# Third batch's list as 19 small blocks, transforms paced eight blocks ahead of their list, gate columns copied by ScalarE, four output buffers

## The chip, the cores and the metric

The kernel runs on one core of one Trainium2 chip. TensorE (PE, with its weight loads as PEld), VectorE (DVE), ScalarE (ACT), GpSimd (POOL) and SyncE (SP) each work through an instruction queue of their own; semaphores order them against each other. SP issues most DMAs, POOL the indirect ones. The metric is the device time of one execution in microseconds (us), lower is better.

## What is computed

A two-dimensional Fourier transform of 8 batches of 2496 tokens by 256 columns, of which the real part goes on; then a mixture of 8 experts, where each token goes through the one expert with the highest gate value. Cut to what matters:

```python
X = np.fft.fft(np.fft.fft(x, axis=1), axis=2).real     # (8, 2496, 256)
x = X.reshape(8 * 2496, 256)
logits = x @ w_gate + modality_bias[modality_id]       # 8 experts
e_idx = np.argmax(logits, axis=1)
gate_w = softmax(logits)[np.arange(N), e_idx]
for e in range(8):
    mask = e_idx == e
    h = np.maximum(x[mask] @ w1[e], 0.0)               # 256 -> 1024
    out[mask] = gate_w[mask, None] * (h @ w2[e])       # 1024 -> 256
```

## The kernel before

**Transforms.** One generator, `stream`, emits all batches in small steps, about 29 to a batch. `fold` adds and subtracts mirrored inputs on VectorE, and `fold_add` squares them on ScalarE (L371, `XM` with `nst`) for a norm, which TensorE sums (L386). `stage1` multiplies into PSUM (`psf`, four buffers) and empties it into `T1`. `stage23` runs over 11 groups: a second transform into `T2`, a third into `psf`, whose 256 columns are emptied into a row tile `rp` (`evac`, L486 on ScalarE and L487 on VectorE) and whose 16 gate columns go to `Lg` (L560). `route` picks each token's expert and its place in that expert's region of the DRAM buffer `xd`. A batch fills four `rp` tiles of up to three groups. Batches 0, 1, 2, 4 and 6 (counted from 0) take them from one pool of `RPB` buffers, the others from a second pool. Each batch's rows go to `xd` by 22 indirect DMAs on POOL (L670, from `rp` and from its mirror `rm`); `paced` and `trickle` spread these between other POOL work.

**Expert blocks.** `block` takes S tokens of one expert, 256 or 128. SP loads the expert's two weight halves (L987, L988; 2.05 MB together; only if the expert differs from the one already in that slot; three slots in turn), the tokens transposed (`xT`, L990) and their output addresses (`ig`, L993). TensorE multiplies into `psm` (L1006); ScalarE takes the ReLU into `H` (L1011), and VectorE the remainder (L1012), each in tiles of 512 columns. TensorE multiplies `H` with the second weights into `pso` (L1024, one buffer). ScalarE scales 128 tokens at a time into an output tile `ob` (L1030, two buffers), and POOL scatters it to the output (L1031). The first half of a block is issued ahead of the second half of the block before it.

**Lists.** First come eight blocks of 256 out of batch 0, one for each expert, while the expert weights are still being prepared ("w", "s" and "b" steps of the string `SEQ` mix weight, transform and block steps; 12 of the 16 half blocks lie in it, the other four behind it). Then come lists: list R holds full blocks of the tokens of batches 0 to R-1 that are not yet taken, as many as are certain to exist whatever the routing: n = (R x 2496 - taken - 8 (S-1)) // S. List 2 has blocks of 128, lists 3 to 8 blocks of 256; what is left goes in a final list of 128. `table` works out on VectorE which expert each block has. With these inputs the numbers of blocks are 15 of 128, then 5, 10, 10, 10, 9 and 10 of 256, then 22 that run of the final list's 24.

**Order.** `fft_moe` emits the transform steps between blocks: `pts` gives, for a count `at` of blocks (in units of 256 tokens), how far the transforms are to be, and `knots` interpolates. Batch b is due one unit before list b begins. A scheduler then fixes each engine's queue from its own estimate of readiness, so what stands in a queue can run ahead of the order in which it was emitted, and a small edit can move rows far from it.

Of the kernel before, what the change touches and what calls it, by code (L numbers as in the profile page):

```python
# [30 lines left out]
ROW = 516  # L31
RW = 516
CH = 3
RPB = 6
RPL = 4
HIP = ()
HIV = ()
# [19 lines left out]
NSLOT = 2  # L57
NS2 = 3
LEAD = 2
EARLY = -1  # L60
FIRST = 2
WAB = 4
WFB = 1
# [162 lines left out]
class Kernel:  # L226
# [288 lines left out]
    def stage23(self, b):  # L515
# [8 lines left out]
        for g in range(G + 1):  # L524
# [19 lines left out]
            if g > 0:  # L544
                T2 = T2s[g - 1]
                ps3 = self.psf.tile([P, 512], F32, name="psf")
                for j, cols in enumerate((slice(0, 145), slice(145, 280))):
                    if hl:
                        for k, (a, w) in enumerate(HL):
                            nc.tensor.matmul(ps3[0:M3, cols], self.e3h[:, a, j, :], T2[:, w, cols], start=k == 0, stop=k == 2)  # L550
                    else:
                        nc.tensor.matmul(ps3[0:M3, cols], self.e3[:, j, :], T2[:, cols], start=True, stop=True)  # L552
                j = (g - 1) % CH
                if j == 0:
                    pool, n = (self.rows, RPL) if b >= SPB and b % 2 else (self.rt, RPB)
                    self.rp.append(pool.tile([M3, CH, RW], I16, name="rp", bufs=n))
                row = self.rp[-1].bitcast(F16)[:, j, 0:512].rearrange("p (h s c) -> p h s c", h=2, c=64)
                seg = ps3[0:M3, 0:288].rearrange("p (s c) -> p s c", c=72)
                self.evac(row, seg[:, :, 0:64], 2.0 ** -20 if hl else self.inv[0][:M3])
                nc.vector.tensor_copy(Lg[:, g - 1], seg[:, 0:3:2, 64:72])  # L560
            yield

    def modality(self):
# [399 lines left out]
    def block(self, S, ti, i, o=0, n=0, ex=None):  # L963
# [62 lines left out]
        gs = p.tile([P, NT], F32, name=f"gs{S}", bufs=3)  # L1026
        V.tensor_scalar(gs, ig[:, :, 1], w2[:, 4 * F:4 * F + 2].bitcast(F32), None, ALU.mult)  # L1027
        for tg in range(NT):
            ob = p.tile([P, D], F32, name="ob", bufs=2)
            self.ob = nc.scalar.activation(ob, po[:, tg, :], AF.Identity, scale=gs[:, tg:tg + 1]).ins  # L1030
            ins = nc.gpsimd.indirect_dma_start(  # L1031
                out=t["out"], out_offset=bass.IndirectOffsetOnAxis(ap=ig.bitcast(I32)[:, tg, 0:1], axis=0),
# [32 lines left out]
def fft_moe(ctx, tc, t):  # L1065
# [32 lines left out]
        next(st, None)  # L1098
    for _ in blk:
        k.paced()  # L1100
        for i in range(3):
            next(st, None)
            k.paced()
    k.started = True

    R0 = FIRST
    size = lambda R: P if R == R0 else 256
    starts, taken = {R0: 0}, k.ntaken
    for R in range(R0, B):
        n = (R * N - taken - E * (size(R) - 1)) // size(R)  # L1110
        starts[R + 1] = starts[R] + n * size(R) / 256
        taken += size(R) * n
    pts = [(0, k.pos)] + [(starts[b] + EARLY, b + 1) for b in range(SPB, B)]
    at = 0
    k.slots = lambda b: int(2 * (starts[b + 1] - LEAD - at))
    tab = k.table(size(R0), False, R0)
    for R in range(R0, B + 1):
        blk, nxt = k.blocks(size(R), tab, R), None
        for _ in blk:
# [3 lines left out]
            if R < B and nxt is None and at >= starts[R + 1] - LEAD:  # L1123
                while k.ready < R:
                    next(st)
                nxt = k.table(256, False, R + 1)
        tab = nxt
    run_all([k.blocks(128, k.table(128, True))])

# [54 lines left out]
```

## Time and profile before

| | |
|---|---|
| median of 3 runs | 1083.2 us (1081.33 to 1083.68) |
| profiled execution | 1081.88 us, span 1080.1 us |
| TensorE busy | 1007.7 us of the span |
| VectorE busy | 552.8 us |
| ScalarE busy | 446.8 us |
| GpSimd busy | 373.3 us |
| moved by DMA | 254.89 MB, mean 236 GB/s |

In the profile a row of a timeline gives start and length in us, engine, line, operation, what it writes and reads, the number of instructions and, in brackets, how long the engine stood idle just before and what released it. Matmuls overlap in the pipeline, so the distance from one start to the next says more than a row's length. A row of the waits gives who waited for whom, the total in us, how often, and the longest. A wait off the path that sets the end costs nothing.

### The profile page before, as it was taken

Reading aid. Unit: us, or ns where it says so; the run is one execution under the profiler, and the core shown is the slowest. Engines: PE = TensorE matmul, PEld = TensorE weight load, DVE = VectorE, ACT = ScalarE, POOL = GpSimd, SP = SyncE. Lnnn points to the kernel's source line nnn. Section 1 sums busy time; section 2 is a strip of 40 time slices with the busy share of each in tenths; the row PEclk is TensorE's granted clock in tenths of the full one; section 3 lists DMA queues with packets and bytes.
Section 4 is the critical chain, followed back from the end, with each engine's and each line's share of the span. In section 5 each row is a group of like instructions: output and inputs, shape, how many; then the busy total and the mean of one; then the engine's idle time right before and its main releaser. Section 6 shows DMA issues by size and latency. Waiting matters only on the chain.

```text
span 1080.1 us, 26648 instructions
## 1 busy us (share of the span) xinstructions
PE 1007.7 (93%) x10128; PEld 910.1 (84%) x10128; DVE 552.8 (51%) x1620; ACT 446.8 (41%) x882; POOL 373.3 (35%) x351
## 2 busy tenths in 40 slices
PE   6776879889998999999999999999999999999996
PEld 5656868779888988889899999888888888899985
DVE  4878888978887442363565334732222222222221
ACT  6755767744644333333443343332323233233221
POOL 0072482861243334343334333345543112121111
PEclk9897989999999999999999999999999999999998
DMA  9667987799497979877878595849976886797663
GB/s 348 246 227 247 308 270 240 260 295 332 135 287 226 305 240 292 225 235 249 252 221 259 178 251 156 244 126 287 298 215 197 244 272 183 222 242 204 163 156 105
DMA packets 156484, 254.89 MB, mean 236 GB/s; under 512 B 118364, under 2 KB 121317, under 8 KB 136125
## 3 DMA queue, kind: packets, MB, share of 16 engines
q1 hardware_dynamic: 136973, 210.96, 66.7%
q0 software_dynamic: 19376, 42.16, 11.8%
q8 instruction: 82, 1.34, 0.5%
q14 instruction: 53, 0.43, 0.1%
HBM read 231.59 MB, written 60.48 MB: 270 GB/s over the span
## 4 chain that ended last, share of the span: by engine, by line
PE 64%; issue 13%; DMA 9%; DVE 5%; ACT 4%; POOL 3%; SPq 1%; POOLq 0%; ACTq 0%; DVEq 0%
PE psm L1006 29%; PE pso L1024 28%; DMA XM<-x 3%; DMA out<-ob,ig 3%; POOL out L1031 2%; PE psf L550 2%; PE psf L532 1%; PE psf L506 1%; ACT wj L812 1%; DVE XM L368 1%; DMA xd<-rp,dsti 1%; PE psf L508 1%; POOL xd L670 1%; DMA wa<-w 1%; DVE w L838 1%
## 5 line engine op out<-in xcount | busy, mean ns | idle before, releaser
L1024 PEld LDWEIGHTS <-H 128*128 128x128 f16 x3864 | 376.1, 98 | 55.7 <-ACT H L1011 10.3
L1031 POOL DMA_INDIRECT out<-ob,ig x161 | 166.6, 1035 | 583.2 <-ACT ob L1030 503.4
L1012 DVE SCALAR_TENSOR_TENSOR H<-psm,H 128x512 f16<-128x512 f32 x322 | 218.4, 686 | 282.7 <-ACT H L1011 281.4
L1006 PE MATMUL psm<-xT,w 128*128 128x256 f16 (+1 forms) x3216 | 315.0, 256 | 13.5 <-DMA xT<-xd 6.7
L1024 PE MATMUL pso<-w,H 128*128 128x256 f16 x2616 | 308.0, 273 | 10.7 <-ACT H L1011 9.0
L1006 PEld LDWEIGHTS <-w 128*128 128x128 f16 x3216 | 268.9, 99 | 41.3 <-issue 11.7
L1011 ACT ACTIVATE H<-psm 128x512 f16<-128x512 f32 x322 | 190.5, 597 | 239.8 <-PE psm L1006 238.7
L1030 ACT ACTIVATE ob<-pso,gs 128x256 f32<-128x256 f32 x161 | 70.7, 471 | 282.1 <-PE pso L1024 239.4
L1006 PE MATMUL psm<-xT,w_y 128*128 128x256 f16 (+1 forms) x1440 | 135.3, 251 | 0.5 <-DVE H L1012 0.4
L670 POOL DMA_INDIRECT xd<-rp,dsti x88 | 104.7, 1190 | 84.5 <-DVE sp_i L863 53.7
L1024 PE MATMUL pso<-w_y,H 128*128 128x256 f16 x1152 | 133.3, 273 | 0.0
L1006 PEld LDWEIGHTS <-w_y 128*128 128x128 f16 x1440 | 117.0, 98 | 11.0 <-issue 1.2
L670 POOL DMA_INDIRECT xd<-rm,dsti x88 | 93.3, 1060 | 28.5 <-issue 25.2
L487 DVE SCALAR_TENSOR_TENSOR T<-psf,T 120x280 f16<-120x280 f32 (+2 forms) x95 | 43.2, 461 | 56.3 <-ACT T L486 55.9
L1027 DVE TENSOR_SCALAR gs<-ig,w 128x2 f32<-128x2 f32 (+1 forms) x67 | 15.2, 227 | 63.2 <-DMA ig<-xd 63.2
L486 ACT ACTIVATE T<-psf 120x280 f16<-120x280 f32 (+2 forms) x95 | 38.6, 421 | 15.4 <-PE psf L532 10.2
L812 ACT ACTIVATE wj<-wa 128x1024 f16<-128x1024 f32 x32 | 34.3, 1072 | 9.5 <-DMA wa<-w 9.4
L550 PE MATMUL psf<-T,pack 120*117 120x145 f16 x330 | 31.8, 224 | 4.8 <-DVE T L487 3.0
L368 DVE TENSOR_TENSOR XM<-XM 128x1280 f32<-128x1280 f32 (+2 forms) x18 | 24.1, 1338 | 23.2 <-DMA XM<-x 23.2
L552 PEld LDWEIGHTS psf<-T,pack 120*117 120x117 f32 x132 | 19.4, 188 | 17.0 <-ACT T L482 11.2
L552 PE MATMUL psf<-T,pack 120*117 120x145 f32 (+1 forms) x132 | 23.4, 300 | 11.1 <-ACT T L482 7.5
L532 PE MATMUL psf<-pack,T 128*120 128x144 f16 (+1 forms) x330 | 32.2, 229 | 1.3 <-DVE Lg L560 1.3
(197 smaller groups left out, 772.8 us busy)
## 6 DMA issues: line engine op xcount, KB each, us to landing
w<-w SPq DMA_DIRECT2D x67, 1028.0 KB
w<-w SPq DMA_DIRECT2D x67, 1024.0 KB
w_y<-w SPq DMA_DIRECT2D x30, 1028.0 KB
w_y<-w SPq DMA_DIRECT2D x30, 1024.0 KB
XM<-x SPq DMA_DIRECT2D x14, 1280.0 KB
wa<-w SPq DMA_DIRECT2D x16, 1024.0 KB
out<-ob,ig POOLq DMA_INDIRECT x161, 6.3
w<-w_x SPq DMA_DIRECT2D x2, 1028.0 KB
```

The source lines that it names most:

```text
L487: self.mark = self.nc.vector.scalar_tensor_tensor(dst[:, 1], ps, scale, dst[:, 0], ALU.mult, ALU.subtract).ins
L532: nc.tensor.matmul(oh, T1[h][:, a, g, :], self.m2h[h][:, w], start=h + k == 0, stop=h * k == 2, skip_group_check=True)
L550: nc.tensor.matmul(ps3[0:M3, cols], self.e3h[:, a, j, :], T2[:, w, cols], start=k == 0, stop=k == 2)
L552: nc.tensor.matmul(ps3[0:M3, cols], self.e3[:, j, :], T2[:, cols], start=True, stop=True)
L670: i = self.nc.gpsimd.indirect_dma_start(out=self.t["xd"], out_offset=bass.IndirectOffsetOnAxis(ap=at, axis=0), in_=row, in_offset=None, bo ...
L812: nc.scalar.activation(jk, x, AF.Square, accum_out=st[:, i:i + 1])
L1006: l1 = nc.tensor.matmul(ps[:, q, :], w1v[:, h, kt, ft], xT[:, xs, :], start=k == 0, stop=k == 5).ins
L1011: nc.scalar.activation(H[:, 0, f0:f0 + NF, :], ps, AF.Relu)
L1012: self.mark = V.scalar_tensor_tensor(H[:, 1, f0:f0 + NF, :], ps, 0.0, H[:, 0, f0:f0 + NF, :], ALU.max, ALU.subtract).ins
L1024: nc.tensor.matmul(po[:, tg, :], H[:, hh, ft, tg * P:(tg + 1) * P], w2v[:, wh, ft, :], start=k == 0, stop=k == 23)
L1030: self.ob = nc.scalar.activation(ob, po[:, tg, :], AF.Identity, scale=gs[:, tg:tg + 1]).ins
L1031: ins = nc.gpsimd.indirect_dma_start(out=t["out"], out_offset=bass.IndirectOffsetOnAxis(ap=ig.bitcast(I32)[:, tg, 0:1], axis=0), in_=ob, i ...
```

## The change

Four edits of the kernel and the settings that go with them:

- Lists below number 4 use blocks of 128 (`SMALL`), so list 3 does as well as list 2. By the formula it has 19 blocks where it had 5 of 256, and the lists behind it have 6, 9, 10, 10 and 10, the final one 23, of which 21 run.
- Batch b is due eight units before list b+1 begins (`AHEAD`), where it was due one unit before list b began. Behind `SEQ`, one transform step follows each half block of the first eight, where three did.
- The gate columns are copied out of PSUM by ScalarE.
- `ob` has four buffers; the pool of row tiles has five where it had six.

```diff
-RPB = 6
+RPB = 5
...
-EARLY = -1
+AHEAD = 8
+SMALL = 4
...
-                nc.vector.tensor_copy(Lg[:, g - 1], seg[:, 0:3:2, 64:72])
+                nc.scalar.copy(Lg[:, g - 1], seg[:, 0:3:2, 64:72])
...
-            ob = p.tile([P, D], F32, name="ob", bufs=2)
+            ob = p.tile([P, D], F32, name="ob", bufs=4)
...
     for _ in blk:
         k.paced()
-        for i in range(3):
-            next(st, None)
-            k.paced()
+        next(st, None)
+        k.paced()
...
-    size = lambda R: P if R == R0 else 256
+    size = lambda R: P if R < SMALL else 256
...
-    pts = [(0, k.pos)] + [(starts[b] + EARLY, b + 1) for b in range(SPB, B)]
+    pts = [(0, k.pos)] + [(starts[b + 1] - AHEAD, b + 1) for b in range(SPB, B)]
...
-                nxt = k.table(256, False, R + 1)
+                nxt = k.table(size(R + 1), False, R + 1)
```

In the changed file the lines behind the settings are numbered one higher. Two places in ScalarE's queue show how the order moved. The first is where the third of the first eight blocks is put out (`ob` with `gs_1750`); `H_1798` is the ReLU of the block behind it, `w_1_107` a half of a prepared weight, `wj` a weight norm, `T_1576` and the like results of the second transform. Before:

```order
L837 ACTIVATE w_1_107<-wa,wsc 128x2048
L542 COPY T_1576<-psf 120x280
L486 ACTIVATE rp<-psf,xsc 117x256
L542 COPY T_1591<-psf 120x280
L812 ACTIVATE wj,wst<-wa 128x1024
L1030 ACTIVATE ob<-pso,gs_1750 128x256 x2
L1011 ACTIVATE H_1798<-psm 128x512
L812 ACTIVATE wj,wst<-wa 128x1024
L1011 ACTIVATE H_1798<-psm 128x512
```

The same place with the change:

```order
L487 ACTIVATE rp<-psf,xsc 117x256
L543 COPY T_1591<-psf 120x280
L1031 ACTIVATE ob<-pso,gs_1750 128x256 x2
L1012 ACTIVATE H_1798<-psm 128x512 x2
L487 ACTIVATE rp<-psf,xsc 117x256
L543 COPY T_1605<-psf 120x280
L1012 ACTIVATE H_1798<-psm 128x512
L475 ACTIVATE XM<-Pt,xsc 128x640
L475 ACTIVATE XM<-Qt,xsc 128x640
L813 ACTIVATE wj,wst<-wa 128x1024
L487 ACTIVATE rp<-psf,xsc 117x256
L561 COPY Lg<-psf 117x16 x2
```

The next block's ReLU stands right behind the two outputs in both; the weight norm that parted its first two tiles has moved behind the third, and copies of gate columns now stand in the queue, two at a time, behind the row tiles.

The second place is late in list 2, where the transforms of batch 5 stand between small blocks; `H_4511` is the ReLU of the list's twelfth block before, `H_4596`, `H_4719` and `H_4862` those of its last three with the change, and `T_6202` and `T_7345` the first of that batch's second transform. Before:

```order
L486 ACTIVATE T_6202<-psf 120x280
L486 ACTIVATE T_6282<-psf 120x280
L486 ACTIVATE T_6303<-psf 120x280
L486 ACTIVATE rp<-psf 117x256 x2
L486 ACTIVATE T_6412<-psf 120x280
L486 ACTIVATE rp<-psf 117x256
L371 ACTIVATE XM,nst<-XM 128x1280
L486 ACTIVATE T_6499<-psf 120x280
L486 ACTIVATE T_6520<-psf 120x280
L1011 ACTIVATE H_4511<-psm 128x512 x2
L1030 ACTIVATE ob<-pso,gs_4646 128x256
L486 ACTIVATE T_6625<-psf 120x280
```

With the change:

```order
L487 ACTIVATE T_7345<-psf 120x280
L487 ACTIVATE T_7524<-psf 120x280
L487 ACTIVATE T_7588<-psf 120x280
L487 ACTIVATE T_7700<-psf 120x280
L372 ACTIVATE XM,nst<-XM 128x1280
L1012 ACTIVATE H_4596<-psm 128x512 x2
L1031 ACTIVATE ob<-pso,gs_4676 128x256
L487 ACTIVATE T_7758<-psf 120x280
L372 ACTIVATE XM,nst<-XM 128x1280
L1012 ACTIVATE H_4719<-psm 128x512 x2
L1031 ACTIVATE ob<-pso,gs_4819 128x256
L1012 ACTIVATE H_4862<-psm 128x512 x2
```

Ahead of the first block shown stand four results and one set of squares, where six results, three row tiles and the squares stood; the next result and the second squares lie a block further on, and the row tiles have moved behind the blocks shown.

## The prediction

> **What bounds the kernel now.** I read first the page's forty slices, then the busy time by stage, then who waited for whom, and last the timeline at the waits. Durations and sums stand against the profiled execution: 1081.88 us, of which its span is 1080.1 us. The median of the runs shown, 1083.2 us, lies 1.3 us above it.
>
> ```profile
> PE   6776879889998999999999999999999999999996
> DVE  4878888978887442363565334732222222222221
> ...
> 0.00:100.00 100.00, 67.85 (x365) 56.40 (x366) 67.88 (x220) 64.05 (x128) 27.89 (x28) 0.88 0.73 261
> 100.00:240.00 140.00, 122.32 (x1117) 107.93 (x1117) 120.28 (x371) 90.03 (x167) 77.94 (x60) 0.93 0.88 277
> 240.00:340.00 100.00, 92.62 (x1279) 88.19 (x1277) 86.63 (x306) 51.06 (x112) 28.21 (x24) 0.98 0.82 242
> 340.00:985.00 645.00, 642.28 (x6274) 580.18 (x6272) 255.31 (x681) 215.68 (x432) 222.70 (x223) 1.00 0.81 235
> 985.00:1080.10 95.10, 82.63 (x1104) 77.37 (x1101) 22.71 (x45) 25.97 (x47) 16.52 (x17) 0.96 0.56 149
> ```
>
> In the slices, of 27 us each, TensorE is at eight or nine tenths from the ninth on, and VectorE is at seven to nine from the second to the thirteenth. A row of the stages gives a stage, its length, the busy time of TensorE, its weight loads, VectorE, ScalarE and GpSimd, then the granted clock, the DMA share and GB/s. TensorE idles 32.2, 17.7, 7.4, 2.7 and 12.5 us in the five stages. From 340 us on it is the bound, and only its own work counts there. The first stage ends about where the first expert matmul begins; TensorE's rows up to that point are the same in both kernels, so I cost that stage at nothing. What can be won lies between 100 and 340 us: 25.1 us of idle TensorE, and a clock below 1.00 after stops. VectorE is busy 86% and 87% there, so it is the next bound.
>
> **Part 1, more small blocks.** By the planner's formula, 9 blocks of 256 go, and 18 of 128 come in net (19 in the third list, one less in the last).
>
> ```profile
> 934.63 4.09 PE L1006 MATMUL psm<-xT,w_y 128*128 128x256 f16 x36
> ...
> 945.12 2.84 PE L1006 MATMUL psm<-xT,w 128*128 128x128 f16 x48
> ...
> 953.03 2.84 PE L1006 MATMUL psm<-xT,w 128*128 128x128 f16 x48
> ...
> 958.34 2.84 PE L1006 MATMUL psm<-xT,w_y 128*128 128x128 f16 x48
> ```
>
> From one start to the next, a block of 256 takes 945.12 - 934.63 = 10.49 us and a block of 128 takes 958.34 - 953.03 = 5.31 us. Nine times (2 x 5.31 - 10.49) = **+1.2 us**. ScalarE and VectorE handle the same hidden elements per token, in tiles of the same 512 columns.
>
> **Part 2, four output buffers.** With two, a block's outputs wait until those of the block before have landed, and what stands behind them in ScalarE's queue waits too.
>
> ```profile
> ACT ob L1030 <- DMA out<-ob,ig: 26.3, 12, 5.6
> ...
> 155.08 0.47 ACT L1030 ACTIVATE ob<-pso,gs 128x256 f32<-128x256 f32 x1 [5.57 <-DMA out<-ob,ig]
> 156.69 0.47 ACT L1030 ACTIVATE ob<-pso,gs 128x256 f32<-128x256 f32 x1 [1.14 <-DMA out<-ob,ig]
> ...
> 157.71 0.61 PE L1024 MATMUL pso<-w,H 128*128 128x256 f16 x2 [5.03 <-ACT H L1011]
> 159.88 1.01 PE L386 MATMUL psf<-wst,ones 128*128 128x1 f32 x4 [1.56 <-ACT T L542]
> 161.89 2.77 PE L1006 MATMUL psm<-xT,w 128*128 128x256 f16 x12
> ...
> 225.75 0.47 ACT L1030 ACTIVATE ob<-pso,gs 128x256 f32<-128x256 f32 x1 [3.00 <-DMA out<-ob,ig]
> 226.77 0.61 PE L1024 MATMUL pso<-w,H 128*128 128x256 f16 x2 [3.10 <-ACT H L1011]
> 227.49 2.58 PE L1006 MATMUL psm<-xT,w 128*128 128x256 f16 x12
> ...
> 939.55 1.47 PE L1006 MATMUL psm<-xT,w_y 128*128 128x256 f16 x12
> ```
>
> Of the 26.3 us that ScalarE waits for output DMAs, two places reach TensorE. Behind the outputs stands the ReLU of the next block (H), and TensorE stops for 5.03 + 1.56 us and for 3.10 us. After each stop twelve matmuls take 2.77 and 2.58 us instead of 1.47, so the lower clock costs 1.3 and 1.1 us more. Together 12.1 us. With four buffers an output needs only the DMAs of two blocks before. Those were issued at 117.54 and 188.45, over 30 us ahead of the stops, so both waits go. What is late next is VectorE:
>
> ```profile
> 117.54 0.99 POOL L1031 DMA_INDIRECT out<-ob,ig  x1 [28.90 <-ACT ob L1030]
> 188.45 0.97 POOL L1031 DMA_INDIRECT out<-ob,ig  x1 [9.58 <-ACT ob L1030]
> ...
> 157.69 0.69 DVE L1012 SCALAR_TENSOR_TENSOR H<-psm,H 128x512 f16<-128x512 f32 x1 [2.51 <-ACT H L1011]
> ...
> 226.75 1.30 DVE L1012 SCALAR_TENSOR_TENSOR H<-psm,H 128x512 f16<-128x512 f32 x2 [3.94 <-ACT H L1011]
> ```
>
> It stood idle for only 2.51 and 3.94 us of these stops and worked through the rest, and TensorE needs its result as well. So I take **-7 us**, between 0 (VectorE fills the stage anyway) and -12.
>
> The Trainium skill, "TensorE: Matmul & The Clock Gate", section "What's actually happening", says that the array's clock halves after an idle window of about 3.4 us. The trace agrees on the factor of about two, but shows it after the 3.10 us stop as well; by the rule that stop would cost 1.1 us less and the removable total would be 11.0 us.
>
> **Part 3, later transforms.** In the second list TensorE meets transform pieces in tight chains, each piece waiting for ScalarE and VectorE to empty the one before.
>
> ```profile
> 270.47 0.47 PE L550 MATMUL psf<-T,pack 120*117 120x145 f16 x5 [1.23 <-DVE T L487]
> 281.43 0.53 PE L550 MATMUL psf<-T,pack 120*117 120x145 f16 x6 [1.21 <-DVE T L487]
> 319.53 0.61 PE L532 MATMUL psf<-pack,T 128*120 128x144 f16 x6 [1.28 <-DVE Lg L560]
> 328.39 0.38 PE L386 MATMUL psf<-nst,ones 128*128 128x1 f32 x2 [0.61 <-DVE tb_v L908]
> 331.26 0.38 PE L386 MATMUL psf<-nst,ones 128*128 128x1 f32 x2 [2.48 <-ACT XM L371]
> ```
>
> The last three waits, 4.4 us, belong to the sixth batch and to the sum of squares of the seventh. There the new order puts blocks between the pieces: on ScalarE four transform results, the squares, a block, one more result and the other squares, a block, where ten pieces stood between two blocks before. A block is 5.31 us of TensorE's work, more than the longest of these waits. The first two waits lie in the fifth batch, whose pieces still stand about as tight. I take **-5 us** (the three waits and a little of the others), between 0 and -7.4, all idle of the stage. That a chain comes back later is not excluded; I count it with the rivals.
>
> **Part 4, gate columns.** 88 copies leave VectorE and join ScalarE.
>
> ```profile
> L560 DVE COPY Lg<-psf 117x16 f32<-117x16 f32 x88 | 14.2, 161 | 0.0
> L482 ACT COPY T<-psf 128x396 f32<-128x396 f32 x12 | 6.0, 497 | 15.9 <-PE psf L508 15.9
> L482 ACT COPY T<-psf 128x264 f32<-128x264 f32 x12 | 4.6, 387 | 2.9 <-PE psf L508 2.9
> ```
>
> VectorE is freed of 0.161 us a copy. ScalarE's copies of 396 and 264 columns differ by 110 ns in 132 columns, so 16 columns should take some 387 - 248 x 0.83 = 181 ns: an estimate, and 16 us in all. Those of the third and fourth batch, 22, fall mostly between 100 and 240 us: 3.5 us off VectorE, 4.0 us onto ScalarE, which is busy 64% there. If VectorE set the pace the gain would be the whole 3.5 us; if the copies stand before a ReLU they cost up to 2. I take **-1 us**, between -3.5 and +2.
>
> The Trainium skill, "ScalarE: Activation LUTs", section "Rules for kernel authors", gives plain elementwise work to VectorE rather than ScalarE, and so speaks against this edit. Its section "What ACT_TABLE_LOAD costs" prices such an instruction at 186 ns + 0.833 ns a column: 199 ns here, 17.5 us in all, an estimate; the sum would stand.
>
> **Part 5, weight loads.** Routing the reference's inputs gives each list's experts. The third list had five blocks of five experts; now its 19 blocks run through experts 0* 3* 5* 0 3 6* 1* 4* 6 1 4 6 2* 5* 6 2 5 6 3*, a star being a load of 2.05 MB, nine loads. Over all lists there are 66 instead of 63. A load in every block needs 2.05 MB in 5.31 us, 386 GB/s, and the highest rate I see in any 20 us is 338:
>
> ```profile
> 100.00:120.00 20.00, 17.08 (x151) 15.24 (x150) 19.76 (x58) 12.85 (x26) 1.97 (x2) 1.00 1.10 338
> ...
> 1002.00 2.85 PE L1006 MATMUL psm<-xT,w 128*128 128x128 f16 x48 [1.10 <-DMA w<-w]
> 1035.35 2.85 PE L1006 MATMUL psm<-xT,w 128*128 128x128 f16 x48 [1.37 <-DMA w<-w]
> ```
>
> The last list, small blocks with nothing between them, shows the price: two waits, 1.10 and 1.37 us, at its two later pairs of neighbouring loads. The third list has two runs of three and one pair, which by that row is five waits of 1.2 us, 6 us; transform pieces between some of the blocks give part of it back. I take **+3 us**, between 0 (the second list's eight loads caused no wait) and +8.
>
> **Part 6, five instead of six row buffers.** The second batch's last group now needs the first batch's third group scattered.
>
> ```profile
> 78.36 0.47 ACT L486 ACTIVATE rp<-psf,xsc 117x256 f16<-117x256 f32 x1 [0.83 <-PE psf L552]
> ...
> 76.66 0.99 POOL L670 DMA_INDIRECT xd<-rp,dsti  x1 [0.30 <-issue]
> ...
> 93.82 5.46 PE L1006 MATMUL psm<-xT,w 128*128 128x256 f16 x36 [6.69 <-DMA xT<-xd]
> ```
>
> That scatter was issued at 76.66 and the write begins at 78.36, so ScalarE may wait a few us. TensorE then waits 6.69 us for the first gather anyway, which covers it: 0, at most +3.
>
> **Sum.** 1.2 - 7 - 5 - 1 + 3 + 0 = -8.8: 1081.9 - 8.8 = 1073.1 for a profiled execution. Half of the 1.3 us to the median added, I say **1074 us**.
>
> **The rivals.** *The gains are hollow* (14%): VectorE, 86% busy from 100 to 340 us, takes up the freed time, and the static order, rebuilt as a whole by the scheduler, only moves the chains. This is also the case that the change doesn't do what it says: already before, the queues ran the fourth and fifth batch several blocks ahead of their due times. Parts 2 and 3 then give 2 us together, against +1.2 and a little weight wait: 1082 to 1084. For it: VectorE's share. Against it: it stood idle 2.51 and 3.94 us in just those stops.
>
> *The third list starves for weights* (18%): if a load runs at the 235 GB/s of the stage from 340 on, it takes 8.7 us against 5.31. The first load of a run is hidden by the third buffer; the five others cost 3.4 us each, 17 us. With 13 us of gains and 1.2 us of cost: 1081.9 + 1.2 - 13 + 17 = 1087. It decides from about 12 us of waits, 2.4 us a load, a rate of 265 GB/s. For it: the DMA share of 0.81 to 0.88 from 100 to 985 us. Against it: the 1.10 and 1.37 us above, and the second list.
>
> *More is won* (8%): without stops the clock stays full, and most of the 17.7 us between 100 and 240 us goes: about 1061.
>
> **How the numbers follow.** The forecast, 1066 to 1080, has 60%. A measurement of this kernel can tell about 0.2%, 2.2 us, from no change. Faster is the forecast and the last rival, 0.68; the same is the hollow case, 0.14; slower is the starved list, 0.18. The range 1064 to 1088 takes in the bounds of the parts except where all fall on one side.
>
> **What would show it.** Right: ScalarE's wait for output DMAs near zero; no TensorE stop of over 2 us between 120 and 330 us; the second list's chains shorter than 1 us each; blocks of the third list at 5.3 us and waits for w of some 3 us in all. Wrong: TensorE's waits on H moved to VectorE as releaser with the stage from 100 to 240 us as long as before; waits for w in the third list above 10 us; ScalarE waiting for xd scatters at a row write; or new chains in the sixth or seventh batch.

## The result, and the profile after

| | before | after |
|---|---|---|
| median | 1083.44 us (1081.33 to 1086.48) | 1098.03 us (1095.73 to 1102.31) |
| profiled execution | 1081.88 us, span 1080.1 us | 1099.11 us, span 1097.3 us |
| ratio to before | 1 | **1.0137**, 95% interval 1.0096 to 1.0178 |

The forecast was 1074 us, faster. The change is **slower**, by some 15 us, and the time lies 10 us above the range's upper end. The sign was wrong.

The stages of after, in the same columns as in the prediction (stage, length, busy time of TensorE, its weight loads, VectorE, ScalarE and GpSimd, granted clock, DMA share, GB/s):

```profile
0.00:100.00 100.00, 67.34 (x353) 55.45 (x354) 65.94 (x194) 63.38 (x148) 28.35 (x28) 0.90 0.72 252
100.00:240.00 140.00, 117.80 (x1022) 103.64 (x1021) 112.02 (x332) 88.25 (x171) 70.53 (x54) 0.89 0.78 256
240.00:340.00 100.00, 91.28 (x1274) 86.52 (x1272) 79.25 (x272) 51.53 (x125) 19.90 (x18) 1.00 0.85 258
340.00:985.00 645.00, 637.05 (x6620) 580.26 (x6618) 263.54 (x693) 225.70 (x473) 230.99 (x232) 1.00 0.84 242
985.00:1097.30 112.30, 99.30 (x1305) 92.98 (x1302) 27.12 (x53) 30.48 (x55) 19.36 (x20) 0.96 0.60 160
```

From 100 to 240 us TensorE idles 22.2 us where it idled 17.7, at a clock of 0.89 where it had 0.93: the stage in which 12 us of stops were to go has got worse. VectorE there has fallen from 120.28 to 112.02 us of work; 3.4 us of that are the 21 gate copies that it made in this stage before, and the rest has slid backwards, out of the stage. A landmark shows it better than the sums: the third block of the second list began at 248.7 us before and begins at 261.2 us now. From 340 to 985 us another 5.2 us of idle time have come in.

Rows chosen from the waits of after. Each row says which engine waited for which, then the total in us, how often, and the longest; the first four are TensorE's, the next four ScalarE's, and the last is VectorE's between 100 and 261 us:

```profile
PE psf L387 <- ACT Lg L561: 11.1, 2, 6.1
PE psm L1007 <- DMA w<-w: 7.5, 3, 3.4
PE psm L1007 <- DVE H L1013: 4.6, 2, 4.4
PE psm L1007 <- DMA w_y<-w: 3.0, 1, 3.0
...
ACT Lg L561 <- DVE rp L488: 19.7, 32, 2.5
ACT Lg L561 <- DVE tb_t L925: 9.6, 1, 9.6
ACT rp L487 <- DMA xd<-rp,dsti: 9.1, 3, 6.5
ACT ob L1031 <- DMA out<-ob,ig: 3.7, 1, 3.7
...
DVE rm L208 <- DMA xd<-rm,dsti: 13.8, 2, 9.6
```

The wait that part 2 was about has gone nearly as forecast: 3.7 us where it was 26.3. In its place ScalarE waits 29.3 us at the gate copies (L561). TensorE waits 11.1 us for two of these copies, but only the longer of its two waits, 6.07 us, goes back to a copy's wait for VectorE. The other, at 87 us, belongs to the row buffers of part 6: the copies ahead of it ran without a wait of their own, behind a row write that had waited for a scatter:

```profile
86.18 0.84 ACT L487 ACTIVATE rp<-psf,xsc 117x256 f16<-117x256 f32 x2 [6.51 <-DMA xd<-rp,dsti]
86.91 0.47 ACT L561 COPY Lg<-psf 117x16 f32<-117x16 f32 x2
...
87.14 1.01 PE L387 MATMUL psf<-wst,ones 128*128 128x1 f32 x4 [4.98 <-ACT Lg L561]
```

The timeline at the longest stop (start, length, engine, line, operation, tiles, and in brackets the idle time ahead with what ended it) shows the chain, first VectorE, then ScalarE, then TensorE, and last the second such stop:

```profile
139.95 0.17 DVE L208 COPY rm<-tail 117x4 int32<-117x4 int32 x1 [9.59 <-DMA xd<-rm,dsti]
142.18 0.87 DVE L488 SCALAR_TENSOR_TENSOR rp<-psf,xsc,rp 117x256 f16<-117x256 f32 x2
...
132.59 0.47 ACT L487 ACTIVATE rp<-psf,xsc 117x256 f16<-117x256 f32 x1
142.67 0.17 ACT L561 COPY Lg<-psf 117x16 f32<-117x16 f32 x1 [9.61 <-DVE tb_t L925]
143.15 0.60 ACT L1012 ACTIVATE H<-psm 128x512 f16<-128x512 f32 x1
...
142.90 0.59 PE L387 MATMUL psf<-wst,ones 128*128 128x1 f32 x2 [6.07 <-ACT Lg L561]
...
220.97 0.17 DVE L208 COPY rm<-tail 117x4 int32<-117x4 int32 x1 [4.22 <-DMA xd<-rm,dsti]
221.05 0.68 DVE L1013 SCALAR_TENSOR_TENSOR H<-psm,H 128x512 f16<-128x512 f32 x1
...
221.79 2.72 PE L1007 MATMUL psm<-xT,w 128*128 128x256 f16 x12 [4.41 <-DVE H L1013]
```

Reading the first: VectorE stands 9.59 us until a buffer for mirror rows (`rm`, three of them) has been scattered. The remainder of a row tile (L488) is behind it in VectorE's queue. ScalarE has written the row (132.59), and its next instruction is the copy of 16 gate columns out of the same PSUM tile, which is released by VectorE (the profile names `tb_t`, a VectorE instruction that ran in between these remainders, at 142.59). It stands 9.61 us, and the ReLU of a block stands behind it. TensorE runs dry for 6.07 us. At 220.97 a ReLU remainder is directly behind another mirror-row copy. So in the profiled executions the two stops of before, at 157 and 226 us, that waited for output DMAs are replaced by two, at 143 and 222 us, that wait for the scatter of mirror rows.

### The profile page after: what moved, and what is told of

Same layout as the page of the kernel before. It is cut to its first block, busy times and chain, and to the rows that moved or that the text cites. A ratio compares the mean times of both kernels' runs of the same rounds, so it can differ in the third digit from the quotient of the medians.

```text
span 1097.3 us, 27718 instructions
## 1 busy us (share of the span) xinstructions
PE 1012.8 (92%) x10560; PEld 918.9 (84%) x10560; DVE 547.9 (50%) x1541; ACT 459.3 (42%) x970; POOL 369.1 (34%) x351
## 4 chain that ended last, share of the span: by engine, by line
PE 62%; issue 13%; DMA 10%; DVE 5%; ACT 4%; POOL 3%; SPq 1%; POOLq 0%; DVEq 0%; ACTq 0%
PE psm L1007 28%; PE pso L1025 28%; DMA xd<-rp,dsti 3%; POOL out L1032 2%; DMA w<-w 2%; DMA xd<-rm,dsti 2%; DMA XM<-x 1%; PE psf L551 1%; PE psf L507 1%; PE psf L533 1%; ACT wj L813 1%; POOL xd L671 1%; DMA xT<-xd 1%; PE psf L509 1%; DMA wa<-w 1%
## 5 line engine op out<-in xcount | busy, mean ns | idle before, releaser
L1032 POOL DMA_INDIRECT out<-ob,ig x161 | 163.5, 1016 | 599.9 <-ACT ob L1031 534.9
L1007 PEld LDWEIGHTS <-w 128*128 128x128 f16 x3504 | 272.1, 99 | 39.4 <-issue 9.0
L1007 PE MATMUL psm<-xT,w_y 128*128 128x128 f16 (+1 forms) x1584 | 136.4, 245 | 3.4 <-DMA w_y<-w 3.0
L1007 PEld LDWEIGHTS <-w_y 128*128 128x128 f16 x1584 | 120.6, 99 | 12.1 <-DMA w_y<-w 3.2
L671 POOL DMA_INDIRECT xd<-rp,dsti x88 | 95.8, 1089 | 83.6 <-DVE sp_i L864 55.4
L671 POOL DMA_INDIRECT xd<-rm,dsti x88 | 101.2, 1149 | 34.0 <-issue 24.6
L488 DVE SCALAR_TENSOR_TENSOR T<-psf,T 120x280 f16<-120x280 f32 (+2 forms) x95 | 42.7, 460 | 45.1 <-ACT T L487 40.6
L1028 DVE TENSOR_SCALAR gs<-ig,w 128x1 f32<-128x1 f32 (+1 forms) x73 | 16.0, 219 | 60.4 <-DMA ig<-xd 60.4
L551 PEld LDWEIGHTS <-pack 120*117 120x117 f16 x330 | 26.8, 132 | 11.0 <-issue 10.4
L533 PE MATMUL psf<-pack,T 128*120 128x144 f16 x330 | 31.8, 229 | 1.2 <-ACT Lg L561 0.8
L538 PE MATMUL psf<-m2u,T 128*120 128x280 f32 x88 | 25.0, 410 | 4.7 <-ACT T L483 2.3
```

What stands on the lines that cost most here:

```text
L488: self.mark = self.nc.vector.scalar_tensor_tensor(dst[:, 1], ps, scale, dst[:, 0], ALU.mult, ALU.subtract).ins
L533: nc.tensor.matmul(oh, T1[h][:, a, g, :], self.m2h[h][:, w], start=h + k == 0, stop=h * k == 2, skip_group_check=True)
L671: i = self.nc.gpsimd.indirect_dma_start(out=self.t["xd"], out_offset=bass.IndirectOffsetOnAxis(ap=at, axis=0), in_=row, in_offset=None, bo ...
L1007: l1 = nc.tensor.matmul(ps[:, q, :], w1v[:, h, kt, ft], xT[:, xs, :], start=k == 0, stop=k == 5).ins
L1032: ins = nc.gpsimd.indirect_dma_start(out=t["out"], out_offset=bass.IndirectOffsetOnAxis(ap=ig.bitcast(I32)[:, tg, 0:1], axis=0), in_=ob, i ...
```

## The experiments

They ran in five sets, each beside runs of the kernel before on the same chip, and the chips differ: there the kernel before took 1083.0, 1084.2 and 1086.9 us on three, 1114.4 (e5 to e8) and 1118.9 us (e13 to e16) on two. Ratios are always to the kernel before beside it.

### The copies: e1, e2, e3, e16

e1 is the changed kernel with the copies back on VectorE.

```diff
-                nc.scalar.copy(Lg[:, g - 1], seg[:, 0:3:2, 64:72])
+                nc.vector.tensor_copy(Lg[:, g - 1], seg[:, 0:3:2, 64:72])
```

> The changed kernel with the gate columns copied by VectorE again. Theory A (ScalarE's copies wait for VectorE's remainder of the same rows, 29 us of ScalarE idle, and TensorE waits 11 us behind them): 1087 to 1091 us against 1098, the waits of TensorE on Lg gone. Theory B (five row buffers: ScalarE waits 9.1 us for scatters at a row write) and theory C (weight loads of the small blocks): still 1095 or more. Theory D (any edit rebuilds the whole order, gains and losses by chance): somewhere within 5 us of 1098 with new waits elsewhere.

Measured: 1091.6 us, ratio 1.0072 (1.0051 to 1.0092). The second list's third block starts at 248.8 us, as before the change. So the copies are worth 1.0137 / 1.0072 = 1.0065, about 7 us, and half of the loss remains without them. TensorE's waits for weights are 13.5 us in e1, 6.6 of them from 340 to 500 us, where they were 2.5 us before.

e3 is the kernel before with the copies on ScalarE and nothing else.

```diff
-                nc.vector.tensor_copy(Lg[:, g - 1], seg[:, 0:3:2, 64:72])
+                nc.scalar.copy(Lg[:, g - 1], seg[:, 0:3:2, 64:72])
```

> The kernel before with this one edit: gate columns copied by ScalarE, behind the remainder. Theory A: 1089 to 1093 us against 1083. Theories B and C: 1081 to 1085. Theory D: anything from 1078 to 1090, with the stops at other places than Lg.

Measured: 1102.83 us, ratio 1.0172 (1.0152 to 1.0192): by the ratio 18.6 us for one changed line. Its waits, ScalarE's over the whole run and VectorE's from 100 to 264 us, are nearly those of after, row by row:

```profile
ACT Lg L560 <- DVE rp L487: 19.9, 29, 1.4
ACT Lg L560 <- DVE tb_t L924: 9.4, 1, 9.4
...
DVE rm L207 <- DMA xd<-rm,dsti: 13.6, 2, 9.3
```

The second list's third block starts at 264.3 us, 15.6 us later than before, so most of the loss arises ahead of it.

e2 is the changed kernel, e16 the kernel before, each with the copy on ScalarE and put ahead of VectorE's remainder, so that no copy waits for VectorE.

```diff
-                self.evac(row, seg[:, :, 0:64], 2.0 ** -20 if hl else self.inv[0][:M3])
-                nc.scalar.copy(Lg[:, g - 1], seg[:, 0:3:2, 64:72])
+                sc = 2.0 ** -20 if hl else self.inv[0][:M3]
+                nc.scalar.activation(row[:, 0], seg[:, :, 0:64], AF.Identity, scale=sc)
+                nc.scalar.copy(Lg[:, g - 1], seg[:, 0:3:2, 64:72])
+                self.mark = nc.vector.scalar_tensor_tensor(row[:, 1], seg[:, :, 0:64], sc, row[:, 0], ALU.mult, ALU.subtract).ins
```

> The changed kernel with the copies still on ScalarE, but put between its own row write and VectorE's remainder, so that they no longer wait for VectorE. Theory A: as good as with the copies on VectorE, 1086 to 1091 us, no ScalarE wait of Lg on VectorE. If it is ScalarE's work and not the wait: 1096 or more. Theories B and C: 1095 or more.

> The kernel before with the copies on ScalarE and put between ScalarE's row write and VectorE's remainder, so that no copy waits for VectorE. If the wait for VectorE is the whole cost of part 4, the waits of Lg for rp are gone and the ratio is 0.997 to 1.003 (the prediction's term was -1 us). If moving the copies reorders the batch whatever they wait for, VectorE still stops for mirror rows or new stops come, and the ratio is above 1.005.

Measured: e2 1097.42 us, ratio 1.0133 (1.0113 to 1.0153); e16 1121.2 us, ratio 1.0017 (0.999 to 1.0043). In both, ScalarE's waits at the copies for the remainder are gone. In e16 a smaller wait the other way round has come, since the remainder now follows the copy:

```profile
DVE rp L562 <- ACT Lg L561: 12.9, 12, 3.3
DVE rm L207 <- DMA xd<-rm,dsti: 11.5, 4, 7.4
```

Alone, then, the copies cost 1.72% behind the remainder and 0.17% ahead of it, though on different chips: that their wait for VectorE is the dear part of e3 is supported. In the changed kernel it did not save the time. e2's early loss is gone (third block of list 2 at 248.9 us), but it loses as much further on: from the second to the fourth block of list 3 it takes 23.0 us (347.6 to 370.7), where e1 takes 12.5. More transform pieces stand between the blocks there, and TensorE waits for a sum of squares:

```profile
370.20 0.59 PE L387 MATMUL psf<-nst,ones 128*128 128x1 f32 x2 [4.08 <-ACT XM L372]
```

So it is not shown that the copies' waits make the 7 us in the changed kernel: without these waits it was expected at 1086 to 1091 us.

### The mirror-row buffers: e5, e9, e12

If the 9.6 us stop of VectorE is what makes the copies dear, a fourth mirror-row buffer should cure it. It fits with five row buffers and two output buffers. e5 is e3 with it, and e12 the kernel before with it and the copies where they were; the lines below are their buffer edit. e9 is the changed kernel with it and, to make room, with two output buffers again.

```diff
-RPB = 6
-RMB = 3
+RPB = 5
+RMB = 4
```

> The kernel before with the gate columns copied by ScalarE, four mirror-row buffers instead of three and, to make room, five row buffers instead of six. Theory M (in the order that this edit gives, VectorE stops 9.3 us for a mirror-row buffer whose scatter has not landed, and ScalarE's copies stop behind it): 1088 to 1093 us against 1102.8 with three, and VectorE's wait for xd<-rm between 100 and 264 us under 3 us instead of 13.6. Theory A (the copies' wait for VectorE costs wherever VectorE is late): 1098 or more, and ScalarE's waits of Lg on VectorE stay near 20 us.

> The changed kernel with a fourth buffer for mirror rows, paid for by going back to two output buffers; ScalarE still copies the gate columns, the third list still has small blocks. Theory M (a copy is dear because VectorE, for which it waits, itself stops some 10 us for a mirror-row buffer): the 9.6 us wait of ScalarE for tb_t and the 9.6 us wait of VectorE for the scatter of mirror rows go, the second list's third block starts near 249 instead of 261 us, and the ratio to the kernel before falls from 1.0137 to 1.005 to 1.009, the cost of the third list. The output-buffer wait of some 26 us on ScalarE comes back and costs at most 2 us, as it did beside the other stops. Rival N (each copy's own wait is the cost, wherever VectorE stands): the sum of ScalarE's waits at the copies stays near 30 us and the ratio stays at 1.011 or above. Rival O (the output buffers do carry a gain of 7 us): the ratio is above 1.015.

> The kernel before with five row buffers and four mirror-row buffers, nothing else. Theory M: VectorE's waits for mirror-row buffers (10.6 us over the run before, none of them reaching TensorE for long) fall below 3 us, and the time by 0 to 5 us: 0.995 to 1.000, so it may beat the kernel before. Rival: these waits were idle VectorE time that nothing needed, and the ratio is that of five row buffers alone, 0.997 to 1.001, with the same stops of TensorE.

Measured: e5 1118.88 us, ratio 1.0027 (0.9992 to 1.0061). That looked like proof. e9 1098.12 us, ratio 1.0143 (1.011 to 1.0177): VectorE's longest wait for mirror rows has fallen to 4.1 us, and nothing is won. ScalarE still waits 25.8 us at the copies for the remainder of a row, as expected there if each copy's own wait is the cost. e12 1098.01 us, ratio 1.012 (1.0089 to 1.0151): the buffer counts alone, with no copy moved, cost 13 us. The timeline of e12, ScalarE, then TensorE, shows the first place:

```profile
87.42 0.84 ACT L486 ACTIVATE rp<-psf,xsc 117x256 f16<-117x256 f32 x2 [6.90 <-DMA xd<-rp,dsti]
...
88.69 1.01 PE L386 MATMUL psf<-wst,ones 128*128 128x1 f32 x4 [6.33 <-ACT T L482]
101.52 4.42 PE L1006 MATMUL psm<-xT,w 128*128 128x256 f16 x21 [7.89 <-DMA xT<-xd]
```

ScalarE waits 6.90 us for one of the five row buffers, and the first expert block starts at 101.5 us, where it started at 93.8 before. A second stop follows at 240.7 us: TensorE stands 10.67 us behind an output that waits 11.78 us for its buffer. How can a count of buffers for mirror rows do that? Part of VectorE's queue in e12 against before (rows with - stood there before, rows with + stand there now):

```
 L207 COPY rm<-tail 117x3x2
 L207 COPY rp<-tail 117x2x2
+L207 COPY rm<-tail 117x2x2
 L378 TENSOR_SCALAR xsc<-xeb 128x1
...
 L487 SCALAR_TENSOR_TENSOR rp<-psf,xsc,rp 117x256
 L560 COPY Lg<-psf 117x16
-L207 COPY rm<-tail 117x2x2
 L376 TENSOR_SCALAR web<-psf 128x1
```

The fourth buffer lets a group's mirror rows be made some thirty rows of the queue earlier, and behind that place rows of all five queues stand in another order. An edit of a buffer count here is not always a local edit. And e5, which has the buffers of e12 and the copies on ScalarE besides, has the ratio 1.0027 against e12's 1.012, though on another chip: what the copies cost depends on the order in which they come to stand. The theory that the three mirror-row buffers explain the loss **falls**: their stop is one form in which it shows.

### The buffers: e4, e8, e13

e4 is the kernel before with four output buffers (and the five row buffers that make room), e8 with five row buffers alone, e13 the changed kernel with both undone.

```diff
-RPB = 6
+RPB = 5
...
-            ob = p.tile([P, D], F32, name="ob", bufs=2)
+            ob = p.tile([P, D], F32, name="ob", bufs=4)
```

> The kernel before with four output buffers and, to make room, five row buffers. The prediction's part 2 alone: 1076 us, ScalarE's wait for output DMAs under 4 us instead of 26. Theory B: the row write of the second batch's last group waits some 6 us and takes most of it back: 1080 to 1084. Theories A and C say nothing on it.

> The kernel before with five row buffers instead of six and nothing else. Theory B: 1086 to 1089 us, as with four output buffers and five row buffers (1087.9), with a ScalarE wait of some 6 us for a scatter at a row write near 80 us. If the output buffers were the cause of that: 1082 to 1084.

> The changed kernel with the two buffer edits undone: two output buffers, six row buffers. ScalarE still copies the gate columns; the third list and its pacing are as changed. If the loss before 260 us belongs to the copies (they put the mirror rows of a batch into one run, so that three buffers run out), VectorE still stops 8 to 10 us for a mirror-row buffer near 140 us, the second list's third block starts at 258 us or later, and the ratio is 1.010 or more. If it belongs to five row buffers (the ScalarE wait of 6.5 us at 86 us), that block starts near 250 us and the ratio is 1.000 to 1.006.

Measured: e4 1087.89 us, ratio 1.0038 (1.0015 to 1.0062); e8 1112.99 us, 0.9987 (0.9959 to 1.0015); e13 1151.04 us, 1.0255 (1.0201 to 1.0309). In e4 the wait of ScalarE for output DMAs fell from 26.3 us to the first row here; the other rows are VectorE's and TensorE's at 146 us:

```profile
ACT ob L1030 <- DMA out<-ob,ig: 2.0, 1, 2.0
...
145.52 0.17 DVE L207 COPY rm<-tail 117x4 int32<-117x4 int32 x1 [8.23 <-DMA xd<-rm,dsti]
145.60 0.69 DVE L1012 SCALAR_TENSOR_TENSOR H<-psm,H 128x512 f16<-128x512 f32 x1
...
146.34 2.72 PE L1006 MATMUL psm<-xT,w_x 128*128 128x256 f16 x12 [7.76 <-DVE H L1012]
```

The stop that part 2 removes is there again 11 us earlier, 7.76 us long, with a remainder behind a mirror-row copy instead of a ReLU behind an output. But these two rows stood together before as well, and there VectorE did not wait:

```profile
137.55 0.16 DVE L207 COPY rm<-tail 117x4 int32<-117x4 int32 x1
137.62 1.28 DVE L1012 SCALAR_TENSOR_TENSOR H<-psm,H 128x512 f16<-128x512 f32 x2
```

e17 (below) shows the same stop with two output buffers. So this trace does not show that the new buffers made it. It does show that nothing is won by then: the third block of list 2 starts at 251.6 us in e4, against 248.7 before. e8, on a slower chip, has no loss with five row buffers alone, so the 0.4% of e4 points to the output buffers.

e13 met two conditions for the copies (the third block of list 2 at 275.0 us, the ratio above 1.010; e14 on the same chip has that block at 260.9 us) and missed one: VectorE waits only 2.7 us in all for mirror rows. Against e14 (below), which ran beside it and differs from it in the copies alone, it is 1.0255 / 1.0103 = 1.015 longer. So the copies cost with six row buffers and without the stop for mirror rows too: neither is needed for it.

### The third list and its pacing: e6, e7, e10, e11, e14, e15, e17, e18

e6 is e1 with the third list back in blocks of 256 (`SMALL = 3`). The others but e15 start from the kernel before. e10 has the new pacing alone:

```diff
-        for i in range(3):
-            next(st, None)
-            k.paced()
+        next(st, None)
+        k.paced()
...
-    pts = [(0, k.pos)] + [(starts[b] + EARLY, b + 1) for b in range(SPB, B)]
+    pts = [(0, k.pos)] + [(starts[b + 1] - 8, b + 1) for b in range(SPB, B)]
```

e11 and e17, one kernel run twice, have the small third list alone:

```diff
-    size = lambda R: P if R == R0 else 256
+    size = lambda R: P if R < 4 else 256
...
-                nxt = k.table(256, False, R + 1)
+                nxt = k.table(size(R + 1), False, R + 1)
```

e7, e14 and e18, one kernel run three times, have both of these edits; e15 is e1 with the old pacing.

> The changed kernel with the gate columns on VectorE and the third list in blocks of 256. Theory C (waits for weights in small blocks, 13.5 us in the run with the copies on VectorE against 2.5 before): 1082 to 1085 us against 1091.6, waits for w under 4 us. Theories B and D: 1088 to 1092, since buffers and pacing are the changed ones.

> The kernel before with the third list in blocks of 128 and the transforms paced eight blocks ahead; copies and buffers as before. Theory C: waits for w of 8 to 12 us and 1086 to 1091 us. The prediction's parts 1, 3 and 5 (1.2 - 5 + 3): 1082 us. Theory B (the buffers cause what is left of the loss): 1081 to 1085.

> The kernel before with the new pacing alone: transforms due eight blocks ahead of their list, one transform step instead of three between the first blocks; the third list in blocks of 256. If part 3 of the prediction is right, the chains of the second list are cut and the time falls by 5 us, a ratio of 0.993 to 0.997, with no TensorE wait above 1.3 us between 250 and 340 us. If the pacing only moves the chains, 0.998 to 1.002. If the pacing is what costs in the run with both, 1.004 to 1.008.

> The kernel before with the third list in blocks of 128 alone, pacing as before. If the small list is what costs in the run with both (weights arriving late, two block heads instead of one): 1.004 to 1.008, with some 5 to 13 us of TensorE waits for w or for the blocks' heads between 340 and 480 us, and the same stops as there. If the two only cost together: 0.999 to 1.002. The prediction's terms for it were 1.2 + 3 us: 1.004.

> The same kernel as in e7: the kernel before with the third list in blocks of 128 and the new pacing. Alone, each of the two gave 1.000. If they cost together (the pacing takes the transforms out from between the small blocks, so that weights fall due closer together), the ratio is again 1.004 to 1.009, with waits for w of 4 us or more between 340 and 500 us. If the 1.0068 belonged to the slower chip, 0.998 to 1.002.

> The changed kernel with the copies back on VectorE and the old pacing; four output buffers, five row buffers and the small third list stay. If the 1.0072 of the run with the new pacing came from pacing and small list together, 0.998 to 1.003 here, with waits for w in the third list near 2.5 us as with the small list alone. If four output buffers cost by themselves (1.0038 with the list in blocks of 256), 1.003 to 1.006. If part 2 of the prediction gains at all, below 0.998.

> The kernel of e11 again (the third list in blocks of 128, pacing as before), beside the kernel of e14. If this set falls on a chip where the kernel before takes some 1084 us: 0.998 to 1.002, as in e11. If it falls on one where it takes 1110 us or more: 0.998 to 1.002 if small list and pacing cost only together; 1.005 to 1.010 if the small list costs by itself where the chip is slow, its list 3 then taking 130 us or more instead of 124.

> The kernel of e7 and e14 again (small third list and new pacing). On a chip where the kernel before takes some 1084 us: 1.004 to 1.009, with a wait for w of 4 us or more in the third list, if the two cost together on every chip; 0.998 to 1.002 if it was the slow chips. On a slow chip: 1.006 to 1.012 as before, and the run beside it tells the small list's share.

| run | edit | before beside it | ratio (95% interval) |
|---|---|---|---|
| e10 | pacing | 1084.2 us | 1.0004 (0.9988 to 1.0021) |
| e11 | small list 3 | 1084.2 us | 0.9994 (0.9974 to 1.0013) |
| e17 | the same | 1086.9 us | 0.9956 (0.9942 to 0.997) |
| e18 | both | 1086.9 us | 1.0022 (1.0002 to 1.0042) |
| e7 | both | 1114.4 us | 1.0068 (1.0043 to 1.0092) |
| e14 | both | 1118.9 us | 1.0103 (1.0063 to 1.0144) |
| e6 | after, copies back, list 3 of 256 | 1114.4 us | 1.0015 (0.9989 to 1.004) |
| e15 | after, copies back, old pacing | 1118.9 us | 1.0084 (1.0051 to 1.0117) |

TensorE's rows at the chains of list 2, in e10 and then, from 300 us on, in e11:

```profile
271.77 0.53 PE L550 MATMUL psf<-T,pack 120*117 120x145 f16 x6 [1.01 <-DVE T L487]
282.20 0.53 PE L550 MATMUL psf<-T,pack 120*117 120x145 f16 x6 [1.21 <-DVE T L487]
321.19 0.61 PE L532 MATMUL psf<-pack,T 128*120 128x144 f16 x6 [1.28 <-DVE Lg L560]
332.92 0.38 PE L386 MATMUL psf<-nst,ones 128*128 128x1 f32 x2 [2.48 <-ACT XM L371]
```

```profile
320.44 0.53 PE L550 MATMUL psf<-T,pack 120*117 120x145 f16 x6 [1.02 <-DVE T L487]
...
328.88 0.53 PE L550 MATMUL psf<-T,pack 120*117 120x145 f16 x6 [0.56 <-DVE T L487]
329.52 0.38 PE L386 MATMUL psf<-nst,ones 128*128 128x1 f32 x2
335.06 0.28 PE L386 MATMUL psf<-nst,ones 128*128 128x1 f32 x2
```

The pacing alone leaves the chains as they were, the 1.28 and the 2.48 us to the hundredth. The small list, with the pacing of before, shortens them: the sums of squares at 329.52 and 335.06 wait for nothing, and 1.02 and 0.56 us at other pieces stand in the place of 1.28. TensorE's longest waits for weights in list 3, in e11, in e18 and in e14:

```profile
389.66 2.85 PE L1006 MATMUL psm<-xT,w 128*128 128x128 f16 x48 [1.33 <-DMA w<-w]
```

```profile
425.17 4.48 PE L1006 MATMUL psm<-xT,w 128*128 128x128 f16 x48 [4.49 <-DMA w<-w]
```

```profile
443.80 5.30 PE L1006 MATMUL psm<-xT,w 128*128 128x128 f16 x48 [4.81 <-DMA w<-w]
```

With the small list alone such waits make 2.5 us from 340 to 500 us (1.6 in e17); with the new pacing as well it is one of 4.49 us, the clock is lower in the block behind it (48 matmuls take 4.48 us instead of 2.85; the granted clock is 0.66 from 425 to 430 us), and the gain is gone: 1088.79 against 1083.21 us beside it. That the two cost together is shown for that chip, though the ratio to before, 1.0022, lies between the two that were expected. On the two slower chips no run has the small list alone: e15 has it with the old pacing, but with the changed buffers too, and its 1.0084 is above all three ranges expected of it. From 340 to 500 us TensorE idles 13 to 15 us there with the small list (e7, e14, e15) and 6 to 10 without; one wait of some 4.5 us does not explain that, and why it is so stays open. e6, with list 3 back in blocks of 256, waits 2.2 us for weights where e1 waited 13.5, and its 1.0015 is what was expected if waits for weights are what is left of the loss without the copies; its chip is another than e1's.

## Why the prediction was wrong

**What bounds the kernel** was read rightly: the idle time that TensorE gains in after arises ahead of 500 us. The change as a whole divides, by ratios of runs on chips of like speed, into three steps: list and pacing 1.0022 (e18), 2.4 us; the buffers on top 1.0072 / 1.0022 = 1.005, 5.4 us; the copies on top 1.0065, 7 us; together 14.8 us. The forecast for the same steps was -0.8 us (parts 1, 3 and 5), -7 (parts 2 and 6) and -1, so it was off by some 3, 12 and 8 us. The intervals are some 2, 3 and 5 us wide to each side, and the parts do not simply add: the copies alone cost 18.6 us, and pacing and buffers without the small list come to 1.0015 (e6, on a slower chip).

**Part 4, gate columns, is the step that failed outright.** "If the copies stand before a ReLU they cost up to 2" priced the copy's own length. That was right (median 172 ns, forecast 181). What it left out is that the copy reads the PSUM tile that VectorE is reading, is emitted behind VectorE's remainder, and so waits for VectorE, with ScalarE's whole queue behind it: 29 us of waits that stood in no row of before. Measured: +7 us in the change, +18.6 us alone, 1.5% between e14 and e13, against -1. That the waits are what costs is supported for the copies alone (e16, which has none of them, 1.0017); in the changed kernel it stays open, since e2 has none either and is as slow as after. The Trainium skill, "ScalarE: Activation LUTs", section "Rules for kernel authors", gives such work to VectorE for its speed per element. It had the right sign here, but the cost does not lie in the instruction (172 ns on ScalarE, 161 on VectorE).

**Part 2, output buffers, -7 us, is the largest miss of the sum: the wait went, the gain did not come.** Alone it cost 0.4% (e4). "What is late next is VectorE" was the right question, but answered by VectorE's idle time in the old order. For the second stop that time was misread as well: VectorE's 3.94 us of idle time (222.81 to 226.75) cover the whole of TensorE's stop of 3.10 us (223.67 to 226.77), so it didn't work through any of it. In the traces of e4 and after VectorE itself stops, for mirror rows, ahead of the very remainder that TensorE needs. That the edit makes this stop is not shown, since e17 has it with two output buffers. That the time does not come back is: the third block of list 2 starts no earlier than before with four of them (248.8 us in e1, 251.6 in e4, 248.7 before). The least gain allowed for, 0, assumed that no new wait could be longer than the old one. Two signs of being wrong that the prediction named did come in after: TensorE waits for H with VectorE as the releaser, and ScalarE waits for scatters at a row write.

**Part 3, later transforms, -5 us: nothing from the pacing.** e10 measures 1.0004 with the chains in place. That the chains get shorter was right as an observation, but the small third list does it, by 2.8 us of waits in e11, and it was put down to the wrong edit.

**Parts 1 and 5, +1.2 and +3 us, were too dear alone.** The mechanism, waits for weights at neighbouring loads, is there, 1.6 to 2.5 us (3.4 us in after from 340 to 500 us, near the +3); together with the chains that this edit cuts it makes 0.6 to 4.8 us of gain (e11, e17). With the new pacing a single wait is as long as 4.5 us, beyond the 1.10 and 1.37 us that it was sized by.

**Part 6, row buffers, 0, at most +3:** right alone (e8). In after ScalarE does wait 6.5 us for a row tile at 86 us, and the first block starts at 95.9 instead of 93.8 us. "TensorE waits for the first gather anyway" covers most of it; in e12 the same wait moved the start by 7.7 us.

**The rivals.** The slower rival, weights, had a part of it: all waits for weights in after are 10.5 us, 8 more than before, where it had 17 in the third list. Its time, 1087, came near that of the changed kernel without the copies, 1091.6, and the weights waits there, 13.5 us, are large enough for it; only half of them lie in the third list. The hollow rival was right that parts 2 and 3 give next to nothing. No rival spoke of an engine made to wait for another by the moved copy. "The static order, rebuilt as a whole by the scheduler, only moves the chains" was in the hollow rival as a harmless case; the runs show that two changed buffer counts, which rebuild it, cost 13 us with nothing else changed (e12). What the order of after has that makes its parts cost less together than e3 alone is not settled.

## What to carry to other kernels

Before an instruction is moved to another engine, look at what it shares with its neighbours: here the second reader of a PSUM tile put two in-order queues in step, and the price of such a wait is everything that stands behind the waiting instruction, not its own 0.17 us. Where a scheduler lays out every queue, a buffer count or a block size can change the order of the whole program, so a stop that is removed has to be looked for again a few us further on, and each edit has to be timed alone. Here the small third list alone was the best that was found: 0.9994 and 0.9956 of before in two sets, both on chips of the faster kind, so between no change and half a per cent faster there.

## What was not expected of the hardware

- The landing time of an indirect scatter differs between two executions of one program, here on two chips, enough to make or unmake a stop. In e11 and then in e17, the same kernel, GpSimd's issue of a mirror-row scatter, VectorE's next use of such a buffer and TensorE's long stop stand like this:

```profile
134.93 0.99 POOL L670 DMA_INDIRECT xd<-rm,dsti  x1 [0.30 <-issue]
...
137.68 0.17 DVE L207 COPY rm<-tail 117x4 int32<-117x4 int32 x1
...
157.93 0.61 PE L1024 MATMUL pso<-w,H 128*128 128x256 f16 x2 [5.28 <-ACT H L1011]
```

```profile
134.66 2.93 POOL L670 DMA_INDIRECT xd<-rm,dsti  x1 [0.30 <-issue]
...
145.55 0.17 DVE L207 COPY rm<-tail 117x4 int32<-117x4 int32 x1 [8.82 <-DMA xd<-rm,dsti]
...
146.37 2.72 PE L1006 MATMUL psm<-xT,w_x 128*128 128x256 f16 x12 [8.23 <-DVE H L1012]
```

  The scatters were issued within 0.3 us of the same time, and one stop is 8.82 us long where the other is none. It costs TensorE 8.23 us in the profiled execution of e17, where the stop of e11 at 157.93 us is missing. That execution is the longest of the seven of e17 (1087.62 us), the kernel with the lowest ratio of all. So one profiled execution with such a stop doesn't prove that the order made it. Whether the edits of e3, e4 and the change bring it about in every execution is not shown; their costs rest on the ratios of many runs.
- Chips differ by more than any edit here: the same kernel takes 1083 us on one and 1119 us on another, and the small third list with its pacing, one kernel, costs 0.2% on one (e18) and 0.7 and 1.0% on two others (e7, e14). The time of one 256-column matmul is the same on both kinds (a row of 36 takes 4.09 us in e18 and in e14). Part of what is longer stands in the waits of TensorE in e14, the largest of such rows being:

```profile
PE pso L1024 <- issue: 19.6, 36, 1.3
```

  "issue" is idle time for which the profile shows no releaser. In e14 it makes 28.7 us in 53 short gaps; in e18, the same kernel, there is none, and the span is 43.7 us shorter. In the other profiled runs on the two slower chips it is 16 to 30 us, on the faster ones at most 0.5. What causes these gaps is not shown.
